# A gated linear attention with an MLP behind it: a new order for the first two units of work

## The chip, the cores and the metric

One core of a Trainium2 chip. The time is that of one execution on the device, in microseconds (us). The kernel before takes 531.16 us (median of 4 runs, 530.63 to 531.72). Ratios in this document are the mean time of one kernel's fast runs over the mean of the fast runs of the kernel before in the same rounds, so they are not quite the ratios of the medians that stand beside them.

## The reference, cut to what matters

```python
f = sigmoid(f_logit)                       # q, k, v, f_logit: (4 batches, 8 heads, 768 steps, 48)
for t in range(768):
    state = f[t][:, None] * state + outer(k[t], v[t])
    y[t] = q[t] @ state
x = y with the heads side by side          # (4, 768, 384)
xn = (x - mean) / sqrt(var + 1e-6) * g_ln
out = x + maximum(xn @ w_ch1, 0) @ w_ch2   # 384 -> 1536 -> 384
```

The two MLP weights arrive as 64-bit floats and have to be converted on the chip.

## The kernel before

The 768 steps are cut into 12 units of 64. A unit's attention is a chain over TensorE (transposes of f, k, q; small products), ScalarE (sigmoid, copies out of PSUM), VectorE (two scans, products, statistics) and GpSimd (the inverse root). Its MLP is 12 parts on TensorE: six "ph" parts (first layer) and six "po" parts (second layer). A part takes 2.58 us at full clock. While the MLP of one unit runs, the attention of the next is woven in between its parts. Units and MLPs are counted from 0.

Names in the traces: `tr` is a transpose of f, k or q; `after` and `upto` are the two scans over the decays; `kh` and `qh` are k and q times these scans; `ps`, `py`, `kp` and `pn` are the small products on TensorE; `kept` is the decayed state of the units before; `xn` is the normalised x, `xp` its transposes, and `xt` these times the norm weights (`gain`), which is what the MLP reads.

The weights come in twelve pieces of 768 KB (six of each layer). A ph part needs one w1 piece, the first po parts need the w2 pieces two by two. Each piece passes four engines:

```python
def fetch():                     # SyncE: DMA into a staging tile (3 of them)
    words = stage.tile(..., tag="words")
    nc.sync.dma_start(out=words, in_=src.bitcast(I32))
def read():                      # ScalarE: three passes; upper and units have 2 buffers each
    nc.scalar.activation(out=upper, in_=high, func=AF.Copy, scale=2.0 ** -112)
    nc.scalar.activation(out=units, in_=low, ...)
    nc.scalar.activation(out=units.bitcast(I32), in_=units, ...)
def write():                     # VectorE: three passes, then GpSimd: one add
    nc.vector.tensor_scalar(out=body, in0=upper, ...)            # clamp
    nc.vector.tensor_scalar(out=body, in0=body, ...)             # shift
    nc.vector.scalar_tensor_tensor(out=upper, in0=upper, in1=body, ...)
    nc.gpsimd.tensor_tensor(out=to.bitcast(I32), in0=upper, in1=units, op=ALU.add)
```

The order of the program text is the order on each engine's queue. Before, the first units were ordered by calls like these:

```python
load(0, "f"); load(0, "k"); load(0, "q"); load(0, "v")   # ... = cuts
fetch(); fetch(); load(1, "f" "k" "q" "v"); gain load on SyncE; fetch()
do.attention(0, "gates", "after", "upto", "k", "q", "scores")
...
do.attention(1, "gates", "after");  do.mlp(0)
do.attention(1, "upto"); piece(read); do.mlp(0)
do.attention(1, "k"); piece(write, read); do.mlp(0)
do.attention(1, "q", "scores"); piece(write, read)
...
```

## Time and profile before

| what | value |
|---|---|
| median | 531.16 us |
| span of the profiled run | 528.0 us, TensorE busy 94% |
| mean granted TensorE clock | 0.974 |
| first ph part starts | 29.99 us |
| sixth (last) ph part of MLP 0 starts | 66.36 us |
| first ph part of the third unit's MLP starts | 127.90 us |
| from there to the end | 400.1 us, TensorE full |

The last three rows cut the run into three stretches: **A**, from the start to the sixth ph part (66.4 us); **B**, from there to the third unit's MLP (61.5 us); **C**, the rest (400.1 us). A is the stretch in which loads, conversions and the first attentions hold TensorE up. In B and C TensorE should be full. The lines that show this stand in the prediction.

### The profile page before, as it was taken

The page shows a single profiled execution, that of the slowest core. Times are in us where ns is not written, and L with a number is a line of the kernel's source. Part 1 is how long each engine was busy: PE and PEld are TensorE (multiplying, and loading weights), DVE is VectorE, ACT ScalarE, POOL GpSimd, SP SyncE. Part 2 cuts the span into 40 slices and gives each one's busy share as a digit, 9 for nine tenths or more (in the row PEclk, how much of TensorE's full clock was granted, in tenths as well). Part 3 has the DMA queues.
Part 4 walks back from the last instruction along what each step waited for, and adds up shares of the span by engine and source line. Part 5 has one row for each costly group of instructions (what it writes and reads, how often), then busy time and mean ns, then how long its engine had stood idle before and what let it go on. Part 6 is the DMA issues. An engine that isn't in the chain of part 4 may idle for free.

```text
span 528.0 us, 10900 instructions
## 1 busy us (share of the span) xinstructions
PE 498.3 (94%) x4841; PEld 383.8 (73%) x4841; DVE 202.0 (38%) x286; ACT 129.1 (24%) x255; POOL 39.2 (7%) x53
## 2 busy tenths in 40 slices
PE   4686799999999999999999999999999999999995
PEld 2565687577876876876876876876886886886873
DVE  7754749712612612603612512522522522422000
ACT  2552567002211211211211211211221220320210
POOL 3301424100000000000000000000000000000000
PEclk9777989999999999999999999999999999999998
DMA  7974239341601600600600600610510520000001
GB/s 130 212 230 122 86 115 185 72 89 31 113 2 31 119 2 23 128 1 17 125 12 16 122 15 17 116 21 16 106 30 16 95 42 16 16 2 17 17 1 34
DMA packets 109703, 33.83 MB, mean 64 GB/s; under 512 B 102736, under 2 KB 105808, under 8 KB 109648
## 3 DMA queue, kind: packets, MB, share of 16 engines
q1 hardware_dynamic: 108592, 32.85, 29.8%
q8 instruction: 40, 0.66, 0.5%
q10 hardware_dynamic: 1056, 0.20, 0.2%
q14 instruction: 15, 0.12, 0.1%
HBM read 28.31 MB, written 4.72 MB: 63 GB/s over the span
## 4 chain that ended last, share of the span: by engine, by line
PE 86%; DVE 5%; SPq 5%; POOL 1%; ACT 1%; issue 1%; DMA 0%; DVEq 0%; POOLq 0%; ACTq 0%
PE po L685 34%; PE ph L678 34%; PE tr L506 5%; SPq L387 4%; PE py L608 4%; PE py L576 2%; PE ps L586 2%; PE kp L599 2%; PE pn L634 2%; DVE w_0body L478 1%; PE xp L663 1%; POOL w L482 1%; DVE w_0upper L480 1%; DVE w_0body L475 1%; DMA gain<-in_moe_g_ln_dram 0%
## 5 line engine op out<-in xcount | busy, mean ns | idle before, releaser
L678 PE MATMUL ph<-xt,w 128*128 128x256 f32 x864 | 199.4, 387 | 7.7 <-POOL w L482 7.4
L685 PE MATMUL po<-w,h 128*128 128x384 f32 x576 | 192.8, 488 | 0.9 <-POOL w L482 0.9
L678 PEld LDWEIGHTS ph<-xt,w 128*128 128x128 f32 x864 | 165.4, 195 | 33.1 <-POOL w L482 7.8
L685 PEld LDWEIGHTS po<-w,h 128*128 128x128 f32 x576 | 106.7, 190 | 69.0 <-POOL w L482 1.5
L680 ACT ACTIVATE h<-ph 128x512 f32<-128x512 f32 x72 | 42.9, 596 | 171.2 <-PE ph L678 171.2
L690 DVE TENSOR_TENSOR o<-x,po 128x384 f32<-128x384 f32 x24 | 13.3, 553 | 105.2 <-PE po L685 105.2
L520 DVE TENSOR_TENSOR_SCAN after<-gates,ends 128x1040 f32<-128x1040 f32 (+1 forms) x13 | 29.3, 2256 | 39.6 <-ACT gates L539 39.6
L623 DVE BATCH_NORM_STATS2 stats<-x 128x6 f32<-128x384 f32 x24 | 13.0, 544 | 71.5 <-ACT x L619 71.5
L665 ACT ACTIVATE xt<-xp,gain 128x128 f32<-128x128 f32 x72 | 19.9, 374 | 83.7 <-PE xp L663 79.8
L590 DVE TENSOR_TENSOR sc<-ps,causal 128x1024 f32<-128x1024 f32 x12 | 14.7, 1225 | 54.5 <-PE ps L586 54.4
L625 POOL TENSOR_SCALAR rstd<-mv 128x2 f32<-128x2 f32 x12 | 2.8, 235 | 380.3 <-DVE mv L624 380.2
L608 PEld LDWEIGHTS py<-v,sc 64*64 64x64 f32 x768 | 24.4, 139 | 6.7 <-issue 5.8
L532 DVE TENSOR_TENSOR_SCAN upto<-gates,starts 128x1040 f32<-128x1040 f32 (+1 forms) x13 | 28.1, 2158 | 0.4
L619 ACT COPY x<-py 128x384 f32<-128x384 f32 x24 | 10.3, 482 | 68.4 <-PE py L608 68.4
L608 PE MATMUL py<-v,sc 64*64 64x48 f32 x768 | 26.0, 223 | 0.6 <-DVE sc L590 0.3
L556 DVE TENSOR_TENSOR qh<-tr,upto 128x512 f32<-128x512 f32 x24 | 15.4, 685 | 26.8 <-PE tr L506 26.8
L601 ACT COPY kt<-kp 128x512 f32<-128x512 f32 x24 | 12.9, 588 | 38.8 <-PE kp L599 38.8
L506 PE MATMUL tr<-ident,fraw 128*128 128x128 f32 x96 | 14.5, 298 | 4.9 <-DMA fraw<-in_f_logit_dram 4.9
L506 PEld LDWEIGHTS tr<-ident,fraw 128*128 128x128 f32 x96 | 12.5, 155 | 6.5 <-POOL causal L406 4.5
L586 PE MATMUL ps<-qh,kh 48*64 48x64 f32 x768 | 14.4, 227 | 2.7 <-DVE qh L556 2.7
L482 POOL TENSOR_TENSOR w<-w_0upper,w_0units 128x768 int32<-128x768 int32 x7 | 13.8, 1974 | 30.3 <-DVE w_0upper L480 30.3
L556 DVE TENSOR_TENSOR kh<-tr,after 128x512 f32<-128x512 f32 x24 | 15.2, 674 | 1.0 <-PE tr L506 1.0
(88 smaller groups left out, 305.4 us busy)
## 6 DMA issues: line engine op xcount, KB each, us to landing
w_0words<-in_moe_w_ch_dram SPq DMA_DIRECT2D x7, 768.0 KB, 4.3
kraw<-in_k_dram SPq DMA_DIRECT2D x48, 96.0 KB, 3.1
qraw<-in_q_dram SPq DMA_DIRECT2D x48, 96.0 KB, 3.1
v<-in_v_dram SPq DMA_DIRECT2D x48, 96.0 KB, 2.9
out_dram<-o SPq DMA_DIRECT2D x48, 96.0 KB, 2.2
fraw<-in_f_logit_dram SPq DMA_DIRECT2D x46, 96.0 KB, 3.0
w_256words<-in_moe_w_ch_dram SPq DMA_DIRECT2D x1, 768.0 KB, 7.1
w_512words<-in_moe_w_ch_dram SPq DMA_DIRECT2D x1, 768.0 KB, 4.7
```

The costliest lines, as they stand in the source:

```text
L387: engines[b % len(engines)].dma_start(out=loaded[n, name][(b % 2) * T:(b % 2 + 1) * T, b // 2, :, 0:D], in_=src[b, :, n * T:(n + 1) * T, : ...
L482: nc.gpsimd.tensor_tensor(out=to.bitcast(I32), in0=upper, in1=units, op=ALU.add)
L506: nc.tensor.transpose(pt[:, a * P:(a + 1) * P], src[:, g, 2 * a:2 * a + 2].rearrange("p h e -> p (h e)"), ident)
L520: nc.vector.tensor_tensor_scan(out=after.rearrange(flat)[:, c0:c1][:, ::-1], data0=gt[:, c0 + 1:c1 + 1][:, ::-1], data1=ends.rearrange(fla ...
L532: nc.vector.tensor_tensor_scan(out=upto.rearrange(flat)[:, c0:c1], data0=gt[:, c0:c1], data1=st.rearrange(flat)[:, c0:c1], initial=0.0, op ...
L556: nc.vector.tensor_tensor(out=dst[:, segs], in0=pt, in1=by[:, segs, 1:E1], op=ALU.mult)
L586: nc.tensor.matmul(ps[half(b), r, e], lhsT=kh[head_rows(r), seg], rhs=qh[head_rows(r), seg], start=True, stop=True)
L608: nc.tensor.matmul(py[half(b), r, e * D:(e + 1) * D], lhsT=sc[half(b), r, e], rhs=vt[half(b), g, 2 * a + r], start=n == 0 and e == 0, stop ...
L665: nc.scalar.mul(out=xt[:, m, g * P:(g + 1) * P], in_=pt[:, m], mul=gain[:, m:m + 1])
L678: nc.tensor.matmul(ph[:, j], lhsT=w1[:, m, (i + j) * P:(i + j + 1) * P], rhs=xt[:, m], start=m == 0, stop=m == KD - 1)
L680: nc.scalar.activation(out=h[:, i:i + 2], in_=ph, func=AF.Relu)
L685: nc.tensor.matmul(po, lhsT=h[:, i, g * P:(g + 1) * P], rhs=w2[:, i], start=i == 0, stop=i == KF - 1)
```

## The change

Its intent is to fill TensorE's holes in stretch A. The order of the first three units is now written as one list of tokens (`l0v`: load v of unit 0; `f`, `r`, `w`: fetch, read, write of the next weight piece; `a1.k`: a stage of unit 1's attention; `m0`: a part of MLP 0). The steady units have a list too. The diff is shortened, and its comments are added here.

```diff
+START = """
+l0v f l0k l0q f l1k l1f a0.gates l1q a0.after a0.k_across a0.upto
+a0.k f a0.q a0.scores r a0.causal l1v w a0.kt a0.values r a0.stats
+w a1.gates a0.state a0.norm a0.turn m0 r a1.after f a1.k_across f a1.upto
+a1.k a1.q w f f r m0 a1.scores a1.causal a1.kt r a1.values
+f w w a1.stats r f a1.state m0 m0 r m0 w
+a1.norm l2k a1.turn w m0 m1 r f m1 m1 m1 w
+r w r f f r l2f w l3q m1 l2q w
+m0 m1 r l2v m0 w a2.gates m1 a2.after m0 m0 a2.k_across
+a2.upto a2.k m0 a2.q m1 a2.scores ...
+"""
+UNIT = """
+m{m} a{n}.gates a{n}.after
+m{m} a{n}.k_across a{n}.upto
+m{m} a{n}.k
 ...
-    for name in "kqv":
-        load(0, name)
+    nc.scalar.dma_start(out=gain, in_=moe_g_ln.rearrange("(c p) -> p c", p=P))
 ...
+        pk = [across(kr, g) for g in range(G)]     # k's transposes, ahead of the second scan
+        yield "k_across"
         if n:
             scan_upto(slice(0, NS))
 ...
-            if n == NU and part == 2:              # check of the smallest decay
+        if m == NU - 2:                            # now at the end of the eleventh MLP
                 worst = consts.tile([P, 1], FP32)
```

More of the change, by code (lines that the diff above doesn't have):

```diff
@@ L300, in general_path @@
     ctx.close()
+START = """
[7 more added lines that the diff above has]
+m0 m1 r l2v m0 w a2.gates m1 a2.after m0 m0 a2.k_across
+a2.upto a2.k m0 a2.q m1 a2.scores l3k a2.causal l3v l3f a2.kt m1
+a2.values m0 a2.stats a2.state m1 a2.norm m1 a2.turn m1
+"""
[3 more added lines that the diff above has]
+m{m} a{n}.k
+m{m} a{n}.q l{o}f l{o}k l{o}q l{o}v
+m{m}
+m{m} a{n}.scores a{n}.causal a{n}.kt
+m{m}
+m{m} a{n}.values a{n}.stats a{n}.state
+m{m}
+m{m} a{n}.norm
+m{m} a{n}.turn
+m{m}
+"""
 @with_exitstack
@@ L551, in attention, with times @@
         qh = work.tile([P, NS, T], FP32, tag="qh", bufs=2, name=f"qh{n}")
-        for src, dst, by in ((kr, kh, after), (qr, qh, upto)):
-            for g in range(G):
-                pt = across(src, g)
+        def times(dst, pts, by):
+            for g, pt in enumerate(pts):
                 segs = slice(g * HS, (g + 1) * HS)
@@ L557, in attention @@
                                         op=ALU.mult)
-            if dst is kh:
-                yield "k"
+        times(kh, pk, after)
+        yield "k"
+        times(qh, [across(qr, g) for g in range(G)], upto)
         nc.vector.tensor_tensor(out=least, in0=least, in1=total, op=ALU.min)
@@ L693, in mlp @@
             yield
-    class Order:
-        def __init__(self):
-            self.units, self.mlps = {}, {}
-        def attention(self, n, *stages):
-            if n >= NU:
-                return
-            if n not in self.units:
-                self.units[n] = attention(n)
-            for stage in stages:
-                got = next(self.units[n])
-                assert got == stage, (got, stage)
-        def mlp(self, n, parts=1):
-            if n not in self.mlps:
-                self.mlps[n] = mlp(n)
-            for _ in range(parts):
-                next(self.mlps[n])
@@ L716 @@
-    do = Order()
-    def piece(*steps):
-        for step in steps:
-            step()
-            if step is read:
-                fetch()
-    fetch()
-    fetch()
-    for name in "fkqv":
-        load(1, name)
-    nc.sync.dma_start(out=gain, in_=moe_g_ln.rearrange("(c p) -> p c", p=P))
-    fetch()
-    do.attention(0, "gates", "after", "upto", "k", "q", "scores")
-    piece(read)
-    do.attention(0, "causal", "kt", "values")
-    piece(write, read)
-    do.attention(0, "stats")
-    piece(write)
@@ L737 @@
-    do.attention(0, "state", "norm", "turn")
-    do.attention(1, "gates", "after")
-    do.mlp(0)
-    do.attention(1, "upto")
-    piece(read)
-    do.mlp(0)
-    do.attention(1, "k")
-    piece(write, read)
-    do.mlp(0)
-    do.attention(1, "q", "scores")
-    piece(write, read)
-    do.attention(1, "causal", "kt", "values")
-    do.mlp(0)
-    piece(write, read)
-    do.attention(1, "stats", "state", "norm")
-    do.mlp(0)
-    piece(write, read)
-    do.attention(1, "turn")
-    do.mlp(0)
@@ L756 @@
-    for part in range(6):
-        do.mlp(1)
-        piece(write, read)
-        if part == 4:
-            for name in "fkqv":
-                load(2, name)
-    assert not (queue or fetched or opened)
-    for part in range(12):
-        do.mlp(part // 6)
-        if part == 1:
-            do.attention(2, "gates", "after")
-        elif part == 2:
-            do.attention(2, "upto")
-            for name in "fkqv":
-                load(3, name)
-        elif part == 3:
-            do.attention(2, "k")
-        elif part == 4:
-            do.attention(2, "q")
-        elif part == 6:
-            do.attention(2, "scores", "causal", "kt")
-        elif part == 8:
-            do.attention(2, "values", "stats", "state")
-        elif part == 9:
-            do.attention(2, "norm")
-        elif part == 10:
-            do.attention(2, "turn")
@@ L783 @@
-    for m in range(2, NU):
-        n = m + 1
-        for part in range(12):
-            do.mlp(m)
-            if part == 0:
-                do.attention(n, "gates", "after")
-            elif part == 1:
-                do.attention(n, "upto")
-            elif part == 2:
-                do.attention(n, "k")
-            elif part == 3:
-                do.attention(n, "q")
-                for name in "fkqv":
-                    load(n + 1, name)
-            elif part == 5:
-                do.attention(n, "scores", "causal", "kt")
-            elif part == 7:
-                do.attention(n, "values", "stats", "state")
-            elif part == 9:
-                do.attention(n, "norm")
-            elif part == 10:
-                do.attention(n, "turn")
-            if n == NU and part == 2:
-                worst = consts.tile([P, 1], FP32)
-                nc.vector.tensor_reduce(out=worst, in_=least, axis=mybir.AxisListType.X,
-                                        op=ALU.min)
-                pw = one_bank("pw")
-                nc.tensor.transpose(pw[0:1, 0:P], worst, ident)
-                least_one = consts.tile([1, 1], FP32)
-                nc.vector.tensor_reduce(out=least_one, in_=pw[0:1, 0:P],
-                                        axis=mybir.AxisListType.X, op=ALU.min)
-                nc.vector.tensor_scalar(out=small, in0=least_one, scalar1=LEAST, scalar2=None,
-                                        op0=ALU.is_lt)
@@ new lines, with run @@
+    running = {}
+    def run(plan):
+        for token in plan.split():
+            kind, rest = token[0], token[1:]
+            if kind == "a":
+                n, stage = rest.split(".")
+                if int(n) >= NU:
+                    continue
+                if "a" + n not in running:
+                    running["a" + n] = attention(int(n))
+                got = next(running["a" + n])
+                assert got == stage, (got, stage)
+            elif kind == "m":
+                if token not in running:
+                    running[token] = mlp(int(rest))
+                next(running[token])
+            elif kind == "l":
+                load(int(rest[:-1]), rest[-1])
+            else:
+                {"r": read, "w": write, "f": fetch}[token]()
@@ new lines @@
+    run(START)
+    assert not (queue or fetched or opened)
+    for m in range(2, NU):
+        run(UNIT.format(m=m, n=m + 1, o=m + 2))
+        if m == NU - 2:
+            worst = consts.tile([P, 1], FP32)
+            nc.vector.tensor_reduce(out=worst, in_=least, axis=mybir.AxisListType.X, op=ALU.min)
+            pw = one_bank("pw")
+            nc.tensor.transpose(pw[0:1, 0:P], worst, ident)
+            least_one = consts.tile([1, 1], FP32)
+            nc.vector.tensor_reduce(out=least_one, in_=pw[0:1, 0:P], axis=mybir.AxisListType.X,
+                                    op=ALU.min)
+            nc.vector.tensor_scalar(out=small, in0=least_one, scalar1=LEAST, scalar2=None,
+                                    op0=ALU.is_lt)
```

## The prediction

> **What bounds the kernel now.** I read the page first, then a table of stretches (windows), then the timeline of the first 100 us, then the chain that ended last.
>
> ```profile
> PE   4686799999999999999999999999999999999995
> PEclk9777989999999999999999999999999999999998
> DMA  7974239341601600600600600610510520000001
> ...
> L678 PE MATMUL ph<-xt,w 128*128 128x256 f32 x864 | 199.4, 387 | 7.7 <-POOL w L482 7.4
> L685 PE MATMUL po<-w,h 128*128 128x384 f32 x576 | 192.8, 488 | 0.9 <-POOL w L482 0.9
> ```
>
> Rows of 13.2 us slices. From the eighth slice on TensorE is busy in every slice at full clock; only the first seven (up to 92 us) have holes and a lowered clock. The stretches put numbers to it (columns: us; then busy time and count for PE, PEld, DVE, ACT, POOL; clock, DMA share, GB/s).
>
> ```profile
> 0.00:30.00 30.00, 16.43 (x239) 13.37 (x239) 19.80 (x32) 11.48 (x21) 9.76 (x21) 0.83 0.87 172
> 30.00:66.30 36.30, 26.51 (x346) 22.26 (x346) 23.07 (x31) 18.23 (x29) 8.16 (x6) 0.86 0.43 142
> 66.30:92.30 26.00, 25.94 (x108) 21.05 (x109) 17.51 (x18) 17.95 (x30) 10.21 (x6) 0.93 0.74 152
> 92.30:128.06 35.76, 34.84 (x369) 23.05 (x368) 15.96 (x22) 4.46 (x12) 2.73 (x3) 1.00 0.33 62
> 128.06:168.54 40.48, 40.48 (x416) 31.39 (x415) 13.81 (x20) 8.16 (x18) 0.92 (x2) 1.00 0.26 50
> ```
>
> The last line is one steady unit: TensorE 40.48 of 40.48 us. The chain repeats that period from 128.06 us (first matmul of the third unit's MLP) to the end, so nothing outside TensorE can be won there. One MLP part (12 ph or 8 po records in the trace) takes 2.58 us in the chain, 12 parts are 31.0 us, an attention unit is the other 9.5. Up to 128.06 us TensorE has two MLPs (62.0) and three attentions to do (27.4, the first about 1.1 shorter because it has no kept state): 89.4 us at full clock. So 38.7 us are lost before 128.06, nearly all before 66.3. That is all the change can touch.
>
> What holds the start, from the timeline (start, us, engine, line, what; idle before and releaser):
>
> ```profile
> 26.23 0.62 SPq L728 DMA_DIRECT2D gain<-in_moe_g_ln_dram  x1
> ...
> 28.71 1.66 ACT L665 ACTIVATE xt<-xp,gain 128x128 f32<-128x128 f32 x6 [3.96 <-DMA gain<-in_moe_g_ln_dram]
> ...
> 29.99 7.09 PE L678 MATMUL ph<-xt,w 128*128 128x256 f32 x24 [0.33 <-ACT xt L665]
> ...
> 41.04 1.80 POOL L482 TENSOR_TENSOR w<-w_512upper,w_512units 128x768 int32<-128x768 int32 x1 [14.26 <-DVE w_512upper L480]
> 42.90 4.88 PE L678 MATMUL ph<-xt,w 128*128 128x256 f32 x12 [4.94 <-POOL w L482]
> ```
> The reader sees: the MLP starts at 29.99; it then waits 4.94 us for the third weight piece, whose conversion sat behind unit 1's scans and kh on VectorE, and those 12 matmuls then run at 407 ns instead of 215 because the idle time cooled the clock. Unit 1's qh waits for q transposes queued behind that stall until 48.25; so unit 1's output is late too, and part 6 of MLP 0 starts at 66.36.
>
> **What the Trainium skill says.** "TensorE: Matmul & The Clock Gate", Part 1: The HAM clock gate: an idle window of about 3.4 us drops TensorE to half rate, and about 3.4 us of work restore it. The trace agrees: 407 against 215 ns after 5 us idle. So closing a hole pays about 1.5 times its length. "SBUF — State Buffer", Who interferes with whom: a VectorE tensor_scalar in its two-port mode, or a VectorE op with two SBUF inputs, and a GpSimd op lock each other out. The trace agrees: the weight shift takes 0.56 us alone and 2.06 us beside GpSimd's weight add, so back-to-back weight writes repeat every 3.8 us rather than 2.1. "DMA: Bandwidth & Descriptors", Issuing engines are not separate DMA queues: all transfers share 16 engines. The trace agrees in one respect: 96 KB loads of 192-byte rows run at 144 GB/s with full engines (0.68 us each), a 768 KB weight piece at 390 GB/s (2.0 us). So a piece put ahead of k and q delays them.
>
> **The change part by part.** No arithmetic is added or removed; I compared the instruction order of both on each engine and walked it by hand with the durations of the trace.
>
> 1. *Loads.* v0 and weight piece 0 go ahead of k0 and q0: 4 x 0.65 + 2.0 us of DMA time. q0 landed at 10.6 (its transposes waited for it); counted from 1.7 us with 1.1 us to complete, k0 now lands at 12.6, q0 at 15.2. VectorE is ready for q at 13.85, so unit 0 loses about 2 us here: qh ends at 16.6 (was 14.49), py at 22.2 (20.7), xn at 28.6 (27.0). In return piece 0 is read on ScalarE while it is idle.
> 2. *gain on ScalarE's queue.* It lands early, so xt waits only for xp: first ph at 29.6, against 29.99. The 2 us of part 1 eat this wait.
> 3. *f1 transposes and gates before unit 0's norm.* Gates end at 26.9, so the scans run 28.6 to 33.7 (before 31.4 to 36.6): 2.9 us earlier.
> 4. *One ph part, then k1 and q1 transposes, then the second part.* Part 0 cold at 407 ns is 4.9 us: 34.5. k and q transposes to 36.4, kh 35.0 to 36.3, qh to 37.7, kept to 38.8 (before 50.5). Part 1, whose piece has been ready since 28, fills 36.4 to 39.0. That removes the 4.94 us hole and its cold matmuls.
> 5. *VectorE then sets the pace:* piece 2 to 40.9, causal product to 42.4 (after py 40.1 and ps 41.1 on TensorE), piece 3 to 44.8, piece 4 (behind GpSimd, 3.8) to 48.6, stats 50.0, state 51.0, piece 5 53.1, xn (2.3 beside GpSimd) 55.4. TensorE has parts 2, 3, 4 in that time and is done at 53.4. xp, then part 5 at 56.0, where it was 66.36: 10.4 us won.
> 6. *From there TensorE is the bound.* 19 parts of 2.58 and the third attention are 58.5 us; before took 61.7 (a cold start and small holes). ScalarE reads three w2 pieces in a row (2.63 each) late, so the last w2 piece is added at about 85.0, 1.4 us after TensorE wants it. Boundary: 56.0 + 58.5 + 1.4 = 115.9, against 128.06: 12.2 us won.
> 7. *Steady units.* k transposes move before the second scan. TensorE is already full, and the bank count holds (k's two PSUM banks come free about 1.4 us before q's transposes want them): 0.
> 8. *The check of the smallest decay moves to the end of the eleventh unit's MLP.* Before, its transpose stood after three ph parts and was free. Now it directly follows the last po part on TensorE, and its operand comes from VectorE behind the output add:
>
> ```profile
> 491.33 7.93 PE L678 MATMUL ph<-xt,w 128*128 128x256 f32 x36
> 491.53 0.56 DVE L690 TENSOR_TENSOR o<-x,po 128x384 f32<-128x384 f32 x1 [7.07 <-PE po L685]
> 492.00 0.16 DVE L807 TENSOR_REDUCE worst<-least 128x1 f32<-128x16 f32 x1
> ```
> TensorE would stand from 491.3 to 492.25 and do the transpose: a loss of about 0.9 us, in place of 0.1.
>
> Sum: 530.86 - 12.2 + 0.9 = 519.6; I put 519.0, since in part 4 the clock may still be warm from xp.
>
> **Rivals.** *A: the start is hidden anyway.* If the w2 conversions (six pieces at 3.8 us is 22.9 us on VectorE, 15.8 on ScalarE) bind after part 5, the 10 us only turn into waiting for w2: time 524 to 527. For it: before, they ran at exactly 3.8 us apiece to 94.7 with TensorE waiting 0.9 at the end. Against: two are now written before the wait matters, and the w2 transfers no longer trail. *B: the late q0 costs more.* If ScalarE's queue order (weight read before gates) or the early loads push unit 0 by 4 us instead of 2, 522. *C: the clock stays warm,* because TensorE never idles a whole window between 22 and 30 us: part 0 in 2.6 instead of 4.9 and piece 2 earlier: 515 to 517. *D: steady units lose,* if k's held banks stall a ph part by 0.3 us in each of nine: 522. The 40.48 of 40.48 and the bank count speak against it.
>
> **Range and chances.** The hand walk has some 25 dependent steps with 0.1 us of doubt each and two structural doubts of 2 us (clock, w2): 514.5 to 523.5. Faster by over 2% means under 520.2, only 1 us from my value: 0.6. Slower by over 2% would need a deadlock-like wait: 0.01.
>
> **What would show it.** Right: first ph near 29.6, second ph part starting before 37 without a wait on POOL, sixth ph part near 56, third MLP's first matmul near 116, period still 40.5, a hole of 0.9 us before the last MLP whose releaser is VectorE. q0's transposes should wait for DMA to about 15. Wrong: a po part waiting on POOL for more than 2 us (A), ph part 0 after 31.5 (B), ph part 0 in 3 us (C), a period above 40.7 (D).

## The result, and the profile after

The changed kernel takes 523.8 us (median of 4 runs, 522.19 to 525.46); the ratio is 0.9862 (0.9827 to 0.9896). The prediction said 519.0, 514.5 to 523.5: the time lies outside the range by 0.3 us, and the gain is 7.4 us where about 12 were foretold.

The page of the changed kernel, rows of 40 slices (13.0 us each) and the po group:

```profile
PE   2789897999999999999999999999999999999996
PEclk9979999999999999999999999999999999999999
...
L718 PE MATMUL po<-w,h 128*128 128x384 f32 x576 | 195.2, 492 | 3.9 <-POOL w L511 3.9
L711 PE MATMUL ph<-xt,w 128*128 128x256 f32 x864 | 196.2, 383 | 0.5 <-ACT xt L698 0.5
```

Before, the ph group waited 7.4 us on GpSimd's weight adds and the po group 0.9. Now ph waits on none and po waits 3.9. The wait has moved from the first layer's pieces to the second's. The seventh slice (78 to 91 us) of TensorE's row has a 7 where there was a 9.

By stretches, from the starts of the ph groups in the timelines:

| | A | B | C | span |
|---|---|---|---|---|
| before | 66.4 | 61.5 | 400.1 | 528.0 |
| predicted for after | 56.0 | 59.9 | 400.9 | |
| after | 55.9 | 65.0 | 400.6 | 521.5 |

(The predicted C is before's plus step 8's 0.8.) A is right to 0.1 us and C to 0.3. So close a hit in A is partly luck: five profiled runs with the same start lie between 54.8 and 58.2 (table at the end of the experiments). All of the miss is in B: 5.1 us. The timeline of TensorE in B (start, us, engine, line, what, count; in brackets the idle time before and its releaser):

```profile
55.91 15.71 PE L711 MATMUL ph<-xt,w 128*128 128x256 f32 x72
71.45 2.74 PE L718 MATMUL po<-w,h 128*128 128x384 f32 x8
74.03 2.75 PE L711 MATMUL ph<-xt,w 128*128 128x256 f32 x12
76.62 1.45 PE L718 MATMUL po<-w,h 128*128 128x384 f32 x4
79.14 1.56 PE L718 MATMUL po<-w,h 128*128 128x384 f32 x4 [1.06 <-POOL w L511]
80.53 1.04 PE L535 MATMUL tr<-ident,fraw 128*128 128x128 f32 x8
81.41 4.04 PE L718 MATMUL po<-w,h 128*128 128x384 f32 x12
88.27 5.83 PE L718 MATMUL po<-w,h 128*128 128x384 f32 x12 [2.83 <-POOL w L511]
93.94 1.04 PE L535 MATMUL tr<-ident,kraw 128*128 128x128 f32 x8
```

Two holes, 1.06 and 2.83 us, both ended by GpSimd's add of a w2 piece. The 12 po records after the second take 5.83 us where 12 took 4.04 before it. A table of stretches gives the clock at 0.70 from 88.3 to 94.0: it fell to 0.50 about 1.3 us after the matmuls had resumed and stayed there for about 3.4 us, so the hole also cooled TensorE. Together: 1.06 + 2.83 + (5.83 - 4.04) = 5.7 us lost in B, against the 1.4 in the prediction. (Against e2 below, which has none of these holes, B is 6.1 us longer; the other 0.4 is not placed.)

Why that add came so late shows on the other engines (same timeline; DVE is VectorE, POOL GpSimd):

```profile
76.90 2.18 POOL L511 TENSOR_TENSOR w<-w_0upper,w_0units 128x768 int32<-128x768 int32 x1 [2.22 <-DVE w_0upper L509]
...
80.67 0.56 DVE L504 TENSOR_SCALAR w_0body<-w_0upper 128x768 f32<-128x768 f32 x1
80.71 2.20 POOL L511 TENSOR_TENSOR w<-w_0upper,w_0units 128x768 int32<-128x768 int32 x1 [1.62 <-DVE w_0upper L509]
81.27 2.06 DVE L507 TENSOR_SCALAR w_0body<-w_0body 128x768 int32<-128x768 int32 x1
83.43 0.96 DVE L509 SCALAR_TENSOR_TENSOR w_0upper<-w_0upper,w_0body 128x768 int32<-128x768 int32 x1
84.31 2.32 DVE L549 TENSOR_TENSOR_SCAN after<-gates,ends 128x1040 f32<-128x1040 f32 x1
...
84.53 3.68 POOL L511 TENSOR_TENSOR w<-w_0upper,w_0units 128x768 int32<-128x768 int32 x1 [1.63 <-DVE w_0upper L509]
```

The adds of the last three pieces start 3.8 us apart (76.90, 80.71, 84.53): VectorE's shift takes 2.06 us beside GpSimd's add of the piece before. VectorE finishes the last piece and goes straight on to unit 2's first scan, at 84.31. GpSimd's add needs the same piece and a semaphore, and starts at 84.53. The add takes 3.68 us instead of 1.8: it ends 1.6 us after the scan does. In the kernel before, the two met the other way round:

```profile
92.84 1.80 POOL L482 TENSOR_TENSOR w<-w_0upper,w_0units 128x768 int32<-128x768 int32 x1 [1.63 <-DVE w_0upper L480]
93.20 3.62 DVE L520 TENSOR_TENSOR_SCAN after<-gates,ends 128x1040 f32<-128x1040 f32 x1 [0.50 <-ACT gates L539]
```

There the scan waited for its gates, GpSimd was first, and it was the scan that was drawn out (3.62), where nothing on TensorE hung on it. This is what "SBUF — State Buffer", Who interferes with whom, of the Trainium skill says: "Issue order, not op shape, decides who blocks." The two traces agree, 1.80 against 3.68 us for the same add.

### The profile page after: what moved, and what is told of

Same layout as the page of the kernel before. It is cut to its first block, busy times and chain, and to the rows that moved or that the text cites. A ratio compares the mean times of both kernels' runs of the same rounds, so it can differ in the third digit from the quotient of the medians.

```text
span 521.5 us, 10893 instructions
## 1 busy us (share of the span) xinstructions
PE 495.8 (95%) x4841; PEld 380.1 (73%) x4841; DVE 201.0 (39%) x286; ACT 129.6 (25%) x255; POOL 41.4 (8%) x53
## 4 chain that ended last, share of the span: by engine, by line
PE 90%; DVE 4%; DMA 2%; ACT 1%; POOL 1%; issue 1%; ACTq 0%; SPq 0%; DVEq 0%; POOLq 0%
PE ph L711 35%; PE po L718 35%; PE tr L535 6%; PE py L641 5%; PE ps L619 2%; PE py L609 2%; PE kp L632 2%; PE pn L667 2%; PE xp L696 2%; DMA kraw<-in_k_dram 1%; DVE w_0body L507 1%; DMA fraw<-in_f_logit_dram 1%; POOL w L511 1%; DVE w_0body L504 1%; DVE w_0upper L509 1%
## 5 line engine op out<-in xcount | busy, mean ns | idle before, releaser
L718 PE MATMUL po<-w,h 128*128 128x384 f32 x576 | 195.2, 492 | 3.9 <-POOL w L511 3.9
L711 PE MATMUL ph<-xt,w 128*128 128x256 f32 x864 | 196.2, 383 | 0.5 <-ACT xt L698 0.5
L711 PEld LDWEIGHTS ph<-xt,w 128*128 128x128 f32 x864 | 163.2, 192 | 24.5 <-issue 0.9
L549 DVE TENSOR_TENSOR_SCAN after<-gates,ends 128x1040 f32<-128x1040 f32 (+1 forms) x13 | 28.0, 2155 | 34.9 <-ACT gates L568 34.9
L641 PEld LDWEIGHTS py<-v,sc 64*64 64x64 f32 x768 | 23.3, 135 | 6.6 <-issue 5.5
L641 PE MATMUL py<-v,sc 64*64 64x48 f32 x768 | 24.8, 219 | 0.7 <-DVE sc L623 0.7
L511 POOL TENSOR_TENSOR w<-w_0upper,w_0units 128x768 int32<-128x768 int32 x7 | 15.3, 2190 | 35.7 <-DVE w_0upper L509 35.7
L535 PE MATMUL tr<-ident,kraw 128*128 128x128 f32 x96 | 13.7, 288 | 4.7 <-DMA kraw<-in_k_dram 4.5
```

Source lines behind the costliest of these rows:

```text
L535: nc.tensor.transpose(pt[:, a * P:(a + 1) * P], src[:, g, 2 * a:2 * a + 2].rearrange("p h e -> p (h e)"), ident)
L549: nc.vector.tensor_tensor_scan(out=after.rearrange(flat)[:, c0:c1][:, ::-1], data0=gt[:, c0 + 1:c1 + 1][:, ::-1], data1=ends.rearrange(fla ...
L641: nc.tensor.matmul(py[half(b), r, e * D:(e + 1) * D], lhsT=sc[half(b), r, e], rhs=vt[half(b), g, 2 * a + r], start=n == 0 and e == 0, stop ...
L711: nc.tensor.matmul(ph[:, j], lhsT=w1[:, m, (i + j) * P:(i + j + 1) * P], rhs=xt[:, m], start=m == 0, stop=m == KD - 1)
L718: nc.tensor.matmul(po, lhsT=h[:, i, g * P:(g + 1) * P], rhs=w2[:, i], start=i == 0, stop=i == KF - 1)
```

## The experiments

Ten kernels ran, each with correct results and beside runs of the kernel before (medians 531.72, 530.52, 531.18). The changed kernel was not run again beside the experiments. The time of the same kernel scatters by 3 us between runs (the changed kernel 522.2 to 525.5), in e1 by 6, so where less is at stake the stretches of the profiled run decide. The experiments that change one part start from the changed kernel.

**e1_scan_behind_o: the scan starts after GpSimd's last add.**

```diff
-m0 m1 r l2v m0 w a2.gates m1 a2.after m0 m0 a2.k_across
+m0 m1 r l2v m0 w a2.gates m1 m0 m0 a2.after a2.k_across
```

> Edit: unit 2's first scan is put behind the output add on VectorE, so that GpSimd's add of the last w2 piece starts before the scan and not after it. Theory (the scan takes the shared port first): that GpSimd add falls from 3.68 to about 1.8 us, TensorE's wait for it from 2.83 to about 0.95 us, and the 12 po matmuls after it from 5.83 to about 3.9 us if the shorter hole no longer cools the clock. Time 1.9 us (still cold) to 3.9 us (warm) below the changed kernel's 523.8: 520 to 522. Rival (TensorE waits for the piece because its transfer or its read on ScalarE is late): GpSimd's add starts no earlier than 84.5 us and the wait stays above 2.5 us, time 523 to 525. Second rival: the later scan delays k and q of unit 2, giving the gain back: 523 to 525 with a new wait on VectorE before unit 2's q.

Measured: 518.83 us (517.17 to 523.2), ratio 0.9777 (0.9719 to 0.9835). Timeline:

```profile
83.45 1.80 POOL L511 TENSOR_TENSOR w<-w_0upper,w_0units 128x768 int32<-128x768 int32 x1 [1.63 <-DVE w_0upper L509]
85.31 4.14 PE L718 MATMUL po<-w,h 128*128 128x384 f32 x12 [0.96 <-POOL w L511]
86.90 0.55 DVE L723 TENSOR_TENSOR o<-x,po 128x384 f32<-128x384 f32 x1 [3.60 <-PE po L718]
87.38 2.32 DVE L549 TENSOR_TENSOR_SCAN after<-gates,ends 128x1040 f32<-128x1040 f32 x1
```

The add is back at 1.80 us, the hole at 0.96, and the po matmuls behind it run warm (4.14). The first rival (late transfer or read) is out: the add starts 28.6 us after the sixth ph part in both kernels, and only its length and what follows changed. The second rival is there in small: q's transposes wait 0.29 us for kh, and the po part behind them starts 4.12 us after the one before, where the changed kernel has 3.46, so 0.7 us are given back. Stretch B fell from 65.0 to 62.1 us, 2.9 for moving one token: 1.9 from the hole and 1.7 from the clock, less 0.7. The 1.7 is not certain to follow: in e8 the longer hole left the clock warm too. The time fell by more than foretold; this profiled run also had a start that was 1.1 us shorter (A 54.8), so the time alone would overstate the edit.

**e2_spread_w2: the w2 conversions begin earlier and are spread.**

```diff
-a1.norm l2k a1.turn w m0 m1 r f m1 m1 m1 w
-r w r f f r l2f w l3q m1 l2q w
-m0 m1 r l2v m0 w a2.gates m1 a2.after m0 m0 a2.k_across
+a1.norm l2k a1.turn w r f w m0 r f w m1
+m1 r f w m1 r l2f w m1 l3q m1 r l2q w
+m0 m1 l2v m0 a2.gates m1 a2.after m0 m0 a2.k_across
```

> Edit: the reads and writes of the five last w2 pieces are spread among the ph parts from 56 us on instead of lumped behind them. Theory (conversion starts late and in a lump, nothing else is short): all pieces are added by about 79 us, no po part waits on GpSimd, no cold po matmuls; first matmul of the third unit's MLP at 114 to 115.5 instead of 120.9; time 517 to 518.5. Rival A (VectorE and GpSimd at 3.8 us a piece are the bound whatever the order): a po wait of over 2 us stays, 521 to 524. Rival B (ScalarE's reads delay the relus and stall ph parts through the PSUM banks): waits of ph on ACT appear, 520 to 524.

Measured: 518.6 us (516.1 to 519.49), ratio 0.9745 (0.9712 to 0.9778).

```profile
58.23 15.71 PE L711 MATMUL ph<-xt,w 128*128 128x256 f32 x72
73.78 2.74 PE L718 MATMUL po<-w,h 128*128 128x384 f32 x8
76.36 2.75 PE L711 MATMUL ph<-xt,w 128*128 128x256 f32 x12
78.94 2.74 PE L718 MATMUL po<-w,h 128*128 128x384 f32 x8
81.53 1.04 PE L535 MATMUL tr<-ident,fraw 128*128 128x128 f32 x8
82.40 7.91 PE L718 MATMUL po<-w,h 128*128 128x384 f32 x24
90.14 1.04 PE L535 MATMUL tr<-ident,kraw 128*128 128x128 f32 x8
```

No po or ph group has a wait left. B is 58.9 us, 6.1 less than in the changed kernel and within 0.4 of the 58.5 us of bare TensorE work in the prediction's step 6. Rivals A and B are out: the same conversions at the same 3.8 us a piece fit beside the ph parts when they start at 58 us. (The last add, at 79.28, is also over before unit 2's scan starts at 83.28, so the meeting of the two that e1 removes is gone here as well.) The third unit's MLP began at 117.1, not at the 114 to 115.5 expected, because this profiled run had a slow start (A 58.2; q of unit 0 landed late and the first ph part began at 32.4); that is scatter of A and not of the edit, which touches nothing before 53 us.

**e3_check_back: the check of the smallest decay returns to its old place.**

```diff
-        if m == NU - 2:            # behind the eleventh MLP
+        if part == 2:              # of the last MLP, behind its third ph part
```

> Edit: only the check of the smallest decay goes back behind the third ph part of the last MLP. My step 8 (it costs 0.9 us where it is): the hole of 0.73 to 1.0 us before the last MLP goes, time 0.9 us below the changed kernel: 522.9. Rival (that hole lies beside something else, or the clock or output path absorbs it): no difference beyond 0.3 us.

(The edit is shown in short: the last MLP gets a loop over its parts, and the check stands behind the third.) Measured: 523.14 us (521.12 to 524.11), ratio 0.9845 (0.981 to 0.9879). The time is inside the scatter; the trace decides. The changed kernel had

```profile
484.56 0.55 DVE L723 TENSOR_TENSOR o<-x,po 128x384 f32<-128x384 f32 x1 [7.06 <-PE po L718]
485.03 0.16 DVE L759 TENSOR_REDUCE worst<-least 128x1 f32<-128x16 f32 x1
485.25 0.27 PE L761 MATMUL pw<-ident,worst 128*1 128x128 f32 x1 [0.73 <-DVE worst L759]
```

and this kernel has no wait there. C is 399.7 us instead of 400.6: 0.9 us, as foretold. Over all runs C is 399.7 to 400.0 in the three kernels with the check back and 400.5 to 401.0 in the eight changed kernels without it.

**e4_steady_old: k's transposes in their old place in the steady units.**

```diff
-m{m} a{n}.k_across a{n}.upto
-m{m} a{n}.k
+m{m}
+m{m} a{n}.k_across a{n}.upto a{n}.k
```

> Edit: in the steady units only, k's transposes go back behind the third ph part. My step 7 (no effect, TensorE full in both orders): period 40.5 us as before, time within 0.3 us of the changed kernel. Rival (the held PSUM banks cost, or the earlier k gains, a few tenths a unit over nine units): 2 us either way, period 40.2 or 40.7.

Measured: 523.78 us (522.08 to 525.03), ratio 0.9855 (0.9823 to 0.9886). The steady units: TensorE is busy 40.50 of 40.50 us in both orders, C is 400.6 in both. The move is worth nothing, in either direction.

**e6_loads_old: k0 and q0 first.**

```diff
-l0v f l0k l0q f l1k l1f a0.gates
+l0k l0q l0v f f l1k l1f a0.gates
```

> Edit: k0 and q0 are loaded ahead of v0 and the first two weight pieces again, nothing else. My step 1 (the new load order costs unit 0 about 2 us, and this carries through): k and q transposes start at 7 and 9.5 us without a long DMA wait, first ph part 1.5 to 2.5 us earlier (27 to 28 us), sixth ph part as much earlier, time 521 to 522.5 against 523.8 of the changed kernel. Also: the first 55 us should scatter less from run to run (the profiled runs so far began the sixth ph part at 54.8 to 58.2 us, with k0 landing at 11.9 to 13.1). Rival (piece 0 then lands later and its read on ScalarE delays x and kt, so the order is worth nothing): first ph part at 29 to 30 us, time 523 to 525.

Measured: 520.2 us (517.19 to 522.07), ratio 0.9781 (0.9732 to 0.9831). k's transposes started at 7.32 instead of 11.92 us and q's at 9.71 instead of 14.33. But the first ph part began at 30.49, later than 29.39: TensorE waited 2.99 us for f of unit 1 behind py, which held up pn and the copies behind it. That ph part then ran warm (2.83 us where it took 5.46): the clock had fallen to 0.50 at about 22.4 us, during the wait for f, and was back before the ph part began. A came out at 54.3 against 55.9. So the 1.6 us of A are the clock's and not the path's that I had named: the ph part is 2.6 us shorter and starts 1.1 later, and from unit 1's k transposes to the sixth ph part both kernels take 21.1 to 21.3 us. That the old order is better is suggested by the times (520.2 against 523.8, and e11 below) and not shown by the trace. The scatter did not shrink: the four runs span 4.9 us.

**e7_gain_old: the norm weights on SyncE's queue again, behind v of unit 1.**

```diff
-    nc.scalar.dma_start(out=gain, in_=moe_g_ln.rearrange("(c p) -> p c", p=P))
...
+                if token == "l1v":
+                    nc.sync.dma_start(out=gain, in_=moe_g_ln.rearrange("(c p) -> p c", p=P))
```

> Edit: the norm weights are loaded on SyncE's queue behind v of unit 1 again, nothing else. My step 2 (worth 0.4 us of start in itself): their load is then issued about 26.8 us and lands about 29.2; xt of unit 0, which starts at 26.7 in the changed kernel, waits for it, its six pieces end at about 30.9 and the first ph part starts near 30.2 instead of 29.4: sixth ph part and time 0.5 to 1 us later, 524 to 525 (inside the run-to-run scatter of 1.5 us, so the trace decides, not the time). Rival (it is hidden behind the second xp, which waits for xn until 28.0): no wait of xt on the load, first ph part at 29.4.

Measured: 525.94 us (525.29 to 526.73), ratio 0.9907 (0.9871 to 0.9944). The load was issued at 28.13 us, took 3.7 us to land, and

```profile
31.94 1.66 ACT L697 ACTIVATE xt<-xp,gain 128x128 f32<-128x128 f32 x6 [5.13 <-DMA gain<-in_moe_g_ln_dram]
...
33.23 4.79 PE L710 MATMUL ph<-xt,w 128*128 128x256 f32 x12 [4.52 <-ACT xt L697]
```

A is 58.95, 3.0 us more. I expected 0.5 to 1, so this was a miss. In the new order one more weight piece stands ahead of that load on the queue; that this is why it came so late was not tested apart. Leaving the load there would have cost far more than the 0.4 us that it cost before. This move is a part of the change that earns its place.

**e8_q1_behind: q of unit 1 transposed behind the second ph part, the third piece written before it.**

```diff
-a1.k a1.q w f f r m0 a1.scores
+a1.k w f f r m0 a1.q a1.scores
```

> Edit: unit 1's q transposes go back behind the second ph part and behind the write of the third weight piece, as before the change. My step 4 (k and q right behind the first ph part is what pulls the MLP forward): py of unit 1 starts 2.5 to 3 us later (42 instead of 39.2), sixth ph part 2.5 to 3 us later (58.5), time 526 to 527. Rival (VectorE's total is the same, so the order of the two does not matter, or the late w2 conversions absorb it): sixth ph part within 1 us, time 523 to 524.5.

Measured: 526.69 us (524.87 to 528.44), ratio 0.9934 (0.9885 to 0.9982). py of unit 1 starts at 42.56 instead of 39.24, A is 59.0 instead of 55.9: 3.1 us, where 2.5 to 3 were foretold. But not all of it is the edit's: the first ph part began at 30.96 instead of 29.39, before anything that was moved. From unit 1's k transposes to the sixth ph part this kernel takes 23.4 us, where the nine kernels that keep this passage as it was take 21.1 to 21.3. So the edit costs 2.1 to 2.3 us, a little less than foretold. One detail tells about the clock. The hole before the last w2 piece is the same 2.83 us as in the changed kernel, yet

```profile
91.36 4.14 PE L718 MATMUL po<-w,h 128*128 128x384 f32 x12 [2.83 <-POOL w L511]
```

the matmuls after it ran warm, and B is 63.3, shorter by the 1.7 us that the cold ones cost. In e3, e4, e6, e7 and e10 the same hole was followed by 5.83 us. So whether a hole of that length cools the clock varies from run to run.

**e10_gates_old: f of unit 1 transposed behind unit 0's norm.**

```diff
-w a1.gates a0.state a0.norm a0.turn m0 r
+w a0.state a0.norm a0.turn a1.gates m0 r
```

> Edit: unit 1's f transposes and gates go back behind unit 0's norm and its transposes. My step 3 (this makes the scans 2.9 us earlier and thus kh, qh and all behind them): scans start about 31 instead of 27.8 us, k product 2 to 3 us later than 35.4, sixth ph part 1.5 to 3 us later, time 525.5 to 527. Rival (the first cold ph part ends at 34.6 anyway, so the scans have 2.4 us of slack and only the remainder shows): sixth ph part 0.3 to 1 us later, time 524 to 525.

Measured: 524.39 us (523.21 to 525.74), ratio 0.9878 (0.9832 to 0.9924). The scans start at 31.92 instead of 27.81 us, kh at 37.02 instead of 35.44, and A is 57.5 instead of 55.9. So the scans are 4.1 us later, of which 1.6 reach the end of A; the rest was slack behind the first ph part. Unit 0 was late in this run before the edit acts: its k transposes started at 12.59 instead of 11.92 us and its xn at 26.24 instead of 25.54. Less these 0.7 us, about 0.9 us are left for the edit (an estimate). That lies in the rival's range, as the time does, and not in the theory's. The warmer first ph part of this run (3.40 us) hardly matters: the second one waited 1.63 us for kh, which waited for the scans.

**e11_spread_check_loads and e12_f1_early: together.** e11 joins the edits of e2, e3 and e6. e12 adds to it an earlier load of f of unit 1 (`l0k l0q l0v f l1f f l1k`). The diff is of e12 against e11.

```diff
-l0k l0q l0v f f l1k l1f a0.gates l1q a0.after a0.k_across a0.upto
+l0k l0q l0v f l1f f l1k a0.gates l1q a0.after a0.k_across a0.upto
```

> Edit: three together: w2 conversions spread, decay check back behind the third ph part, old order of the first loads. If the parts add: 518.6 (spread alone) - 0.9 - 2 = 515.7. If the late conversions come back as the bound because the sixth ph part is earlier: a po wait on GpSimd of about 1 us, 516.5 to 518. Run-to-run scatter as in the loads run.

> Edit: the combined version (spread conversions, check back, k0 and q0 first) with f of unit 1 loaded ahead of the second weight piece and of k of unit 1. In the combined version and in the one with the old loads TensorE waited 1.6 to 3.8 us for f of unit 1 behind py, which holds pn and with it ScalarE's copies. Theory: f lands about 4.6 us earlier (18 to 20 us), that wait goes, first ph part at 27.5 to 28.5 instead of 28.9 to 30.5, time 1 us below the combined version: 514 to 515. Rival (the second weight piece, now later, delays its conversion and through it xn): first ph part 29 or later, time 515.5 to 517.

Measured: e11 515.55 us (512.76 to 516.04), ratio 0.9696 (0.9648 to 0.9745); e12 515.39 us (515.16 to 516.4), ratio 0.9717 (0.9683 to 0.9752). Both beat both kernels. e11: A 55.3, B 58.9, C 399.9, close to the sum of the parts. In e12 the wait for f is gone, but the rival of that run was right: the second weight piece now lands later, ScalarE waits for it until 22.32 and xn does not come earlier, so nothing is won over e11.

All stretches together:

| kernel | A | B | C | median us |
|---|---|---|---|---|
| before | 66.4 | 61.5 | 400.1 | 531.16 |
| after | 55.9 | 65.0 | 400.6 | 523.8 |
| e1 scan behind the add | 54.8 | 62.1 | 401.0 | 518.83 |
| e2 spread | 58.2 | 58.9 | 400.7 | 518.6 |
| e3 check back | 55.8 | 65.0 | 399.7 | 523.14 |
| e4 steady old | 56.5 | 65.0 | 400.6 | 523.78 |
| e6 loads old | 54.3 | 65.0 | 401.0 | 520.2 |
| e7 gain old | 59.0 | 65.0 | 400.9 | 525.94 |
| e8 q1 behind | 59.0 | 63.3 | 400.9 | 526.69 |
| e10 gates old | 57.5 | 65.0 | 400.5 | 524.39 |
| e11 spread, check, loads | 55.3 | 58.9 | 399.9 | 515.55 |
| e12 the same, f1 early | 54.6 | 58.9 | 400.0 | 515.39 |

B hardly varies between runs, apart from the 1.7 us of the clock in e8: 65.0 in every other kernel that keeps the changed conversions and the place of the scan (e1 moves it), 58.9 in every one that spreads them. The scatter of the times thus comes mostly from A and from the clock after holes. What makes A vary from 54.8 to 58.2 with the same start is settled in part. From unit 1's k transposes to the sixth ph part, nine of the eleven new kernels take 21.1 to 21.3 us (e8 and e10, which edit what comes there, take 23.4 and 23.2), so the variation lies ahead of these transposes: in when the first ph part starts and in how long it is cold. The profiled runs differ in when k0 and q0 land (k's transposes started at 11.9 to 13.1 us) and in the length of the first ph part (4.51 to 5.46 us), but no experiment held one of the two fixed. The mean clock goes with the time: in e8 the two runs near 525 us had 0.993 and the two near 528 had 0.984; in e11, whose B has no hole, the fastest run (512.76) had 0.996 and the other three (515.25 to 516.04) 0.987 or 0.988.

## Why the prediction was wrong, point by point

- **Step 1 (new load order costs unit 0 about 2 us): right at first, too much further on.** qh ended at 17.1 us (foretold 16.6, before 14.5), but xn at 27.90 (foretold 28.6, before 27.0), so 0.9 of the 2.6 us were left by then. q0's transposes started at 14.33 and not at about 15. What the order is worth at the end of A is not shown (e6).
- **Step 2 (norm weights): the direction right, the size wrong.** First ph at 29.39 against 29.6. The 0.4 us is what it cost in the old order; in the new one it would have cost 3.0 (e7).
- **Step 3 (scans from 28.6 to 33.7): right**, 27.81 to 32.99, and 0.8 better; about 0.9 us of A by e10.
- **Step 4 (k and q right behind the first ph part): right.** k's transposes at 34.64 (34.5), second ph part at 36.55 (36.4), unit 1's kept state done at 38.87 (38.8). e8 shows 2.1 to 2.3 us for the q half of it.
- **Step 5 (sixth ph part at 56.0): right**, 55.91, to the tenth by luck: the first ph part was colder (5.46 us) than the 4.9 foretold and started 0.2 us earlier.
- **Step 6 failed.** It said that "the last w2 piece is added at about 85.0, 1.4 us after TensorE wants it". The mechanism, late lumped conversions, was named, also as rival A (524 to 527), but its term was sized at 1.4 us. It measured 5.7: 1.06 for the fourth w2 piece, 2.83 for the last, and 1.8 of cold matmuls after it. Three things were missing from that term, and together they make 5.0 of the 5.1 us by which B was missed. First, step 6 paced the lump by ScalarE's reads, at 2.63 us a piece; it went at the 3.8 us of VectorE and GpSimd taking turns, which rival A had named. The last piece's VectorE passes ended at 84.4 and not at the 83.1 that an add of 1.9 us ending at 85.0 implies: 1.3 us. Second, GpSimd's add then took 3.68 us, because the scan got the port first: 1.9 us; e1 shows that this alone is worth 2.9 us of B, with the cold matmuls that went with it. Third, I charged a hole at its length and left out the cold matmuls behind it: 1.8 us. The prediction itself says that a hole costs about 1.5 times its length; this one cost 1.6 times in six profiled runs and nothing extra in one (e8). e2 shows that the conversions were the whole of it: B fell to 58.9, where step 6's TensorE work alone is 58.5.
- **Step 7 (steady units 0): right**, by e4. **Step 8 (0.9 us for the moved check): right**, by e3.
- **Rivals.** A came true in kind, with its sign (a po part waiting 2.83 us on GpSimd), at 523.8 just below its range. B, C and D did not: the first ph part began at 29.4 and took 5.46 us, and the period stayed at 40.5. Single runs of other kernels show what B and C had in mind: the first ph part began at 32.4 in e2 and took 2.83 us in e6.
- **Slips that do not matter.** The third unit's MLP before starts at 127.90 and not at 128.06, so step 6 foretold 12.0 us and not 12.2. The sum adds 0.9 for step 8, whose own net is 0.8. The loads of 192-byte rows run at 150 GB/s in the stretch where the engines are full (5 to 10 us), not at 144.

The range was too narrow for another reason as well: the walk was for one run, and stretch A varies by 3.4 us between profiled runs with the same start.

## What to carry to other kernels

When a change fills the holes of a pipeline's start, walk on to the next thing that the full engine will ask for: here TensorE reached the second layer's weights while their conversions were still queued behind the work that had been pulled forward. Where two engines share a port, look in the order on each queue at who will be ready first; here the instruction that followed in its own queue without a wait started 0.22 us before the one that needed a semaphore from that engine, and it kept the port. Cutting the run into stretches at fixed milestones, and comparing these instead of the total, told parts of 1 us apart in B and C under a scatter of 3 us. In A, which itself varies by 3.4 us, it took a milestone right before the edit (e8, e10) to keep that variation out of what the edit is worth.

## What the Trainium skill lacked or had wrong

- "SBUF — State Buffer", Who interferes with whom, has the rule (the first to issue holds the port) and the traces bear it out. It lacks who is first when one engine hands over to the other: VectorE's next instruction started 0.22 us before GpSimd's add that waited for the one before it, and the add took 3.68 us instead of 1.80. It also gives no rate for a chain that alternates between the two: 3.8 us a piece, where the VectorE passes alone take 2.1 and the add 1.8.
- "TensorE: Matmul & The Clock Gate", Part 1: The HAM clock gate, puts the cooling at an idle window of about 3.4 us or more. It lacks what a hole of about that length costs. The one before the last w2 piece is 2.83 us long by the matmul records and 3.44 by the weight loads. In six profiled runs the clock fell to 0.50 behind it, 0.5 to 1.3 us after the matmuls had resumed, and stayed there for about 3.4 us (5.83 us for 12 po records); in one it did not fall (4.14 us). The page says that its window runs free of the program, which fits with the spread. The holes of 0.9 to 1.1 us in B were followed by no fall of the clock in any of these traces.
- "DMA: Bandwidth & Descriptors": no page gives the delay of a tiny load among larger ones. The 1.5 KB of norm weights took 2.4 us to land in the kernel before and 3.7 in e7, both from SyncE's queue, and 4.1 from ScalarE's queue in the changed kernel, where nothing waited for it. (The 3.0 us that e7 lost are more than this landing: the load was also issued late, at 28.13 us.)
